# A chunked linear-attention and gated-MLP kernel on one core: 64-bit weights brought to 32 bits by shift, mask and integer add, their range tested on a second load, and an issue order by a finer table of ranks

## The chip, the core and the metric

The kernel runs on one core of a Trainium2 chip. The metric is the device time of one execution in microseconds. Engines: PE is TensorE, DVE VectorE, ACT ScalarE, POOL GpSimd, SP SyncE (here it only issues transfers).

## What is computed

For 4 batches, 8 heads, 768 steps and head size 48, a state of 48 x 48 is carried along:

```python
for t in range(S):
    kt, vt, rt, wt = (k[:, :, t], v[:, :, t], r[:, :, t], w[:, :, t])
    cur = einsum('bhd,bhe->bhde', u[None] * kt, vt)
    y[:, :, t] = einsum('bhd,bhde->bhe', rt, state + cur)
    state = wt[:, :, :, None] * state + einsum('bhd,bhe->bhde', kt, vt)
h = maximum(x @ w_in, 0)                    # x is y as [4, 768, 384], w_in [384, 1024]
conv = sum(conv_w[j] * h[t - 1 + j] for j in 0, 1, 2)
out = (h * sigmoid(conv)) @ w_out           # w_out [1024, 384]
```

`w_in`, `conv_w` and `w_out` arrive as 64-bit floats, the rest as 32-bit ones.

## The kernel before

**Attention.** Each batch is cut into six chunks of 128 steps, 24 in all. `stage_a(n)` loads w, k, r, v of a chunk (192 KB each, in runs of 192 bytes), transposes them on PE (L541), builds running products of w with two scans on DVE (L548, L555), scales k and r by them (L553, L559), and tests w against two bounds on ACT (the guards, L605). `stage_b(n)` makes the scores (L662), masks them by a predicated copy (L666), carries the state (L679, L683, L685) and writes y as a high and a low part into `xT` (L733 or L710, L735 or L711).

**MLP.** `block` takes 384 steps. For each of eight tiles of 128 hidden columns it makes nine products on PE (L755), relu, convolution and gate on ACT and DVE (L767 to L774; the gate is L774), and a high part on ACT and a low part on POOL (L776, L777). Then come three output tiles of 24 products each (L784). There are eight blocks, 64 hidden tiles.

**Weights.** They are used as two 32-bit parts, high and low. They arrive as pairs of 32-bit words, in three groups of `w_in` (`win_pieces`: 384, 384 and 256 columns, each in two halves, one issued by SP and one by ACT) and three of `w_out` (`wout_pieces`). `convert` works on a piece of 128 rows and up to 384 columns; there are 17, 14 wide and 3 of 256 columns. `from_double` takes the exponent (L439 on DVE, L442 on ACT), puts the sign to it (L444, DVE), takes the upper mantissa (L447, DVE), adds the lower word scaled (L450, DVE) and multiplies both on POOL (L453). Then ACT casts the high part (L459) and POOL subtracts for the low one (L460). Raw words lie in the ring of five "gh" slots, in which the hidden tiles lie later, three to a slot.

**The order.** Everything is recorded in `Plan`. `issue` replays it against the durations in `LEN`: whenever an engine is free, it takes the ready operation of lowest rank whose buffers can be had. So each engine's program order is set by ranks. Before, a rank is a formula: `CHUNK` times the chunk, `UNIT` for each hidden tile, `PIECE` for each piece of weights. On the chip the engines run their own lists in order and wait for each other by semaphores.

Of the kernel before, what the change touches and what calls it, by code (L numbers as in the profile page):

```python
# [12 lines left out]
I32 = mybir.dt.int32  # L13
# [11 lines left out]
CHUNK, LEAD, UNIT, DOWN, PIECE = 14.0, 0.0, 5.0, 1.6, 5.0  # L25
FIRST_IN, FIRST_OUT = -10.0, 60.0
AHEAD, GUARD = 10.0, 10.0
# [8 lines left out]
    tr=0.35, kback=0.35, scores=1.1, carried=0.9, state=0.42, y=0.95, mm3=0.53,  # L36
    scan=0.86, small=0.1, pad=0.07, kt=0.47, dg=0.47, cp=0.62, xlo=0.6, sd=0.22, s=0.27,
    stt=0.54, gate=0.47, wts=0.47, wstt=0.47,
    fill=0.25, kh=0.42, guard=0.72, sbd=0.34, xhi=0.49, relu=0.5, mul=0.49, sig=0.43, cast=0.42, out=0.37, exp=0.52,
    z=0.98, diag=1.07, lo=0.97,  # L40
    gather=1.6, carried_rows=1.4, y_rows=1.5,
    load=0.55, issue=0.45, spread=0.64,
)
TAIL = dict(PE=0.22, DVE=0.11, ACT=0.13, POOL=0.07, SP=2.2)
# [66 lines left out]
class Plan:  # L111
# [6 lines left out]
    def op(self, eng, us, f, r=(), w=(), holds=(), moves=0.0, port=False, rank=None):  # L118
        i, deps = len(self.ops), set()
        us = LEN[us] if isinstance(us, str) else us  # L120
# [18 lines left out]
        self.ops.append((eng, us, f, deps, bufs, moves, port, (self.rank if rank is None else rank) + i * 1e-6))  # L139

    def issue(self):
        n = len(self.ops)
        left = [len(o[3]) for o in self.ops]
        users = [[] for _ in range(n)]
        for i, o in enumerate(self.ops):
            for d in o[3]:
                users[d].append(i)
# [5 lines left out]
        for i in range(n):  # L153
            if not left[i]:
                ready[self.ops[i][0]].append((self.ops[i][7], i))
        events, order, t = [], [], 0.0
# [17 lines left out]
        while len(order) < n:  # L174
            for e in engines:
                if free[e] > t:
                    continue
                for k, (_, i) in enumerate(sorted(ready[e])):
                    if places(self.ops[i][4]):
                        break  # L180
                else:
                    continue
                ready[e].remove((self.ops[i][7], i))
                _, us, _, _, _, moves, port, _ = self.ops[i]
                at = t
                if e == "PE" and t < COLD:
                    us *= 1.4
# [5 lines left out]
                free[e] = at + us  # L193
                if moves:
# [5 lines left out]
            assert t < float("inf"), "no order found"  # L200
# [95 lines left out]
def rwkv_conv_moe_kernel(  # L296
# [545 lines left out]
    for n in range(N + 1):  # L842
        if n < N:
# [6 lines left out]
            if f0 < DF:  # L850
                plan.rank = FIRST_IN + PIECE * KT * n
                win_pieces(f0, min(HB, DF - f0), piece, (chunks[n]["w"], 1))
                if n == 0:
                    load_conv()
# [51 lines left out]
```

## Time and profile before

| | |
|---|---|
| runs | 386.19, 386.65, 386.65 us; median 386.65 |
| profiled execution, span | 387.1 us |
| PE busy | 350.6 us (91%), 2790 matmuls |
| DVE, ACT, POOL busy | 281.8, 234.5, 174.6 us |
| HBM read, written | 25.19, 4.72 MB |
| mean granted clock of TensorE | 0.966 |

The span is that of one execution, from its first instruction to its last; it is 0.45 us above the median of the runs. Engines work beside each other, so busy times don't add up. Matmuls overlap: two that follow each other start closer together than one lasts. A row's mean is the length of one instruction; on DVE and ACT too, an instruction that doesn't wait starts some 80 ns before its predecessor's record ends.

### The profile page before, as it was taken

The page shows a single profiled execution, that of the slowest core. Times are in us where ns is not written, and L with a number is a line of the kernel's source. Part 1 is how long each engine was busy: PE and PEld are TensorE (multiplying, and loading weights), DVE is VectorE, ACT ScalarE, POOL GpSimd, SP SyncE. Part 2 cuts the span into 40 slices and gives each one's busy share as a digit, 9 for nine tenths or more (in the row PEclk, how much of TensorE's full clock was granted, in tenths as well). Part 3 has the DMA queues.
Part 4 walks back from the last instruction along what each step waited for, and adds up shares of the span by engine and source line. Part 5 has one row for each costly group of instructions (what it writes and reads, how often), then busy time and mean ns, then how long its engine had stood idle before and what let it go on. Part 6 is the DMA issues. An engine that isn't in the chain of part 4 may idle for free.

```text
span 387.1 us, 7859 instructions
## 1 busy us (share of the span) xinstructions
PE 350.6 (91%) x2790; PEld 320.3 (83%) x2790; DVE 281.8 (73%) x575; ACT 234.5 (61%) x613; POOL 174.6 (45%) x199
## 2 busy tenths in 40 slices
PE   5545978798899999999999999999999999999992
PEld 2435856687688999998999999999999989999992
DVE  4357989999998688578776876688867774656520
ACT  4133766687776565389747663697664725766621
POOL 5265596865785444056443532454544310434320
PEclk9856999899999999999999999999999999999998
DMA  9999984422334354373323447244424130110001
GB/s 150 151 159 179 231 242 98 92 53 49 66 66 99 69 107 78 89 153 85 73 60 75 88 96 143 56 102 94 93 52 94 41 75 10 30 33 20 22 20 69
DMA packets 113571, 34.46 MB, mean 89 GB/s; under 512 B 103069, under 2 KB 110774, under 8 KB 113526
## 3 DMA queue, kind: packets, MB, share of 16 engines
q1 hardware_dynamic: 112852, 32.32, 40.9%
q10 hardware_dynamic: 674, 1.57, 2.0%
q8 instruction: 24, 0.39, 0.4%
q14 instruction: 21, 0.17, 0.1%
HBM read 25.19 MB, written 4.72 MB: 77 GB/s over the span
## 4 chain that ended last, share of the span: by engine, by line
PE 71%; DVE 11%; DMA 5%; issue 3%; SPq 3%; ACT 3%; POOL 2%; ACTq 0%; DVEq 0%; POOLq 0%
PE bank L784 25%; PE bank L755 23%; PE bank L662 6%; PE bank L728 4%; PE bank L541 4%; PE bank L718 4%; PE bank L679 2%; SPq L509 2%; DMA v<-in_v_dram 2%; DMA gh<-in_moe_w_in_dram 2%; PE bank L597 2%; DVE pm L666 1%; DVE a L771 1%; DMA r<-in_r_dram 1%; DVE e L444 1%
## 5 line engine op out<-in xcount | busy, mean ns | idle before, releaser
L755 PE MATMUL bank<-xT,wi 128*128 128x386 f32 x576 | 129.0, 349 | 2.2 <-ACT xT L710 1.7
L784 PE MATMUL bank<-wo,gh 128*128 128x384 f32 x576 | 127.2, 344 | 2.1 <-POOL wo L460 1.7
L777 POOL TENSOR_TENSOR gh<-g,gh 128x384 fp32r<-128x384 f32 x64 | 64.7, 1015 | 114.5 <-ACT gh L776 109.6
L755 PEld LDWEIGHTS bank<-xT,wi 128*128 128x128 f32 x576 | 101.6, 190 | 5.7 <-issue 2.0
L784 PEld LDWEIGHTS bank<-wo,gh 128*128 128x128 f32 x576 | 100.2, 188 | 4.3 <-POOL wo L460 2.0
L769 DVE SCALAR_TENSOR_TENSOR a<-bank,cw,a 128x384 f32<-128x384 f32 x64 | 38.6, 609 | 23.1 <-ACT a L768 22.9
L774 DVE TENSOR_TENSOR g<-bank,a 128x384 f32<-128x384 f32 x64 | 34.8, 549 | 19.0 <-ACT a L773 18.2
L773 ACT ACTIVATE a<-a 128x384 f32<-128x384 f32 x64 | 33.4, 522 | 23.9 <-DVE a L771 23.8
L767 ACT ACTIVATE bank<-bank 128x386 f32<-128x386 f32 x64 | 30.6, 478 | 25.4 <-PE bank L755 24.5
L589 POOL TENSOR_SCALAR_AFFINE_SELECT pm<-dg 128x1024 f32<-128x1024 f32 x24 | 26.2, 1092 | 41.5 <-PE bank L728 39.1
L776 ACT CAST gh<-g 128x384 fp32r<-128x384 f32 x64 | 32.5, 512 | 12.2 <-DVE g L774 12.1
L771 DVE SCALAR_TENSOR_TENSOR a<-bank,cw,a 128x384 f32<-128x384 f32 x64 | 38.8, 611 | 0.8
L666 DVE COPY_PREDICATED pm<-upper,bank 128x512 f32<-128x512 int32 x48 | 33.5, 725 | 5.5 <-PE bank L662 5.2
L768 ACT ACTIVATE a<-bank,cw 128x384 f32<-128x384 f32 x64 | 36.7, 581 | 0.5
L583 POOL TENSOR_TENSOR z<-r,k 128x384 f32<-128x384 f32 x24 | 24.4, 1016 | 12.2 <-DMA r<-in_r_dram 12.2
L548 DVE TENSOR_TENSOR_SCAN kr<-bank,one_end 128x387 f32<-128x387 f32 x24 | 22.9, 956 | 9.2 <-PE bank L541 9.1
L453 POOL TENSOR_TENSOR val<-val,e 128x384 f32<-128x384 f32 (+2 forms) x18 | 16.7, 927 | 19.1 <-DVE val L450 8.0
L585 POOL TENSOR_TENSOR z<-z,ubc 128x384 f32<-128x384 f32 x24 | 24.2, 1008 | 1.2
L662 PEld LDWEIGHTS bank<-kr 48*128 48x128 f32 x288 | 18.4, 188 | 7.0 <-issue 4.1
L662 PE MATMUL bank<-kr 48*128 48x128 f32 x288 | 23.2, 290 | 0.9 <-DVE val L450 0.9
L555 DVE TENSOR_TENSOR_SCAN kr<-bank,dA 128x387 f32<-128x387 f32 x24 | 22.9, 953 | 0.1
L541 PE MATMUL bank<-ident,k 128*128 128x128 f32 x72 | 13.0, 293 | 10.6 <-ACT k L535 10.6
(108 smaller groups left out, 523.7 us busy)
## 6 DMA issues: line engine op xcount, KB each, us to landing
w<-in_w_dram SPq DMA_DIRECT2D x24, 192.0 KB, 3.1
k<-in_k_dram SPq DMA_DIRECT2D x24, 192.0 KB, 3.5
r<-in_r_dram SPq DMA_DIRECT2D x24, 192.0 KB, 3.6
v<-in_v_dram SPq DMA_DIRECT2D x24, 192.0 KB, 3.1
out_dram<-val SPq DMA_DIRECT2D x24, 192.0 KB, 2.0
gh<-in_moe_w_out_dram SPq DMA_DIRECT2D x2, 1152.0 KB, 8.4
last<-kr SPq DMA_DIRECT2D x120, 16.2 KB, 1.8
xT<-xT SPq DMA_DIRECT2D x18, 64.0 KB, 2.4
```

The source lines that it names most:

```text
L662: nc.tensor.matmul(sc[g].t[:, m * L:(m + 1) * L], lhsT=kt(m)[p], rhs=rt(m)[p], start=True, stop=True)
L666: op("DVE", "cp", lambda g=g: nc.vector.copy_predicated(out=pm.t[:, g], mask=upper.unsqueeze(1).to_broadcast([P, NP, L]), data=sc[g].t.rea ...
L755: nc.tensor.matmul(t.t[:, 0:xs.stop - xs.start], lhsT=wi[:, m, a, f * P:(f + 1) * P], rhs=xT[:, x0 + m, c, xs], start=(m == 0 and j == 0), ...
L767: ("ACT", "relu", lambda: nc.scalar.activation(out=h(0, width + 2), in_=h(0, width + 2), func=AF.Relu), [t], [t]),
L768: ("ACT", "mul", lambda: nc.scalar.mul(out=a(), in_=h(1), mul=cw[:, 1, f:f + 1]), [t, "cw"], [a1]),
L769: ("DVE", "stt", lambda: nc.vector.scalar_tensor_tensor(out=a(), in0=h(0), scalar=cw[:, 0, f:f + 1], in1=a(), op0=ALU.mult, op1=ALU.add), ...
L771: ("DVE", "stt", lambda: nc.vector.scalar_tensor_tensor(out=a(), in0=h(2), scalar=cw[:, 2, f:f + 1], in1=a(), op0=ALU.mult, op1=ALU.add), ...
L773: ("ACT", "sig", lambda: nc.scalar.activation(out=a(), in_=a(), func=AF.Sigmoid), [], [a1]),
L774: ("DVE", "gate", lambda: nc.vector.tensor_tensor(out=g.t[:, 0:width], in0=h(1), in1=a(), op=ALU.mult), [t, a1], [g]),
L776: ("ACT", "cast", lambda: nc.scalar.copy(out=part(0)[:, 0:width], in_=g.t[:, 0:width]), [g], [key]),
L777: ("POOL", "lo", lambda: nc.gpsimd.tensor_tensor(out=part(1)[:, 0:width], in0=g.t[:, 0:width], in1=part(0)[:, 0:width].bitcast(F32), op=AL ...
L784: nc.tensor.matmul(acc.t[:, 0:DM], lhsT=part(a)[:, tt * P:(tt + 1) * P], rhs=wo[:, f, c, :], start=(f == 0 and a + c == 0), stop=(f == FT ...
```

## The change

- `convert` no longer goes through the exponent. ACT turns the low word into its top three bits, rounded (a scaled copy to integer), and takes the sign of the high word as 1.0 or -1.0. DVE shifts the high word left by three and masks it (one instruction), and adds the two as integers (another). POOL multiplies by the sign. Cast and low part are as before. Per piece DVE has two instructions instead of four, ACT three instead of two, POOL two as before.
- This holds for magnitudes between 2^-127 and 2. So `in_range` loads all weights a second time (six loads, through the "gh" ring), masks and compares the exponent's upper bits on DVE, and sums up what differs on ACT. The sum joins the guards' flags; if it isn't zero, the general path converts the weights in the old way and computes everything again.
- All halves of `w_in` are issued by SP. `conv_w` is converted as before.
- Ranks come from a table, `RANKS`, with one number for each step of each chunk, piece, hidden tile and output tile. `LEN` has other durations, and PE's operations are charged for a change of their form (`SWITCH`).

```diff
-CHUNK, LEAD, UNIT, DOWN, PIECE = 14.0, 0.0, 5.0, 1.6, 5.0
+DOWN = 1.6
+RANKS = dict(
+    load=[-152.0, -79.7, -8.9, -117.1, -75.2, -21.5, 44.6, 131.8, 85.2, -38.1, -95.7, 157.3, 110.7, 49.5, -13.0,
...
+    range=[150.7, 286.2, 238.8, 120.4, 266.7, 215.2],
...
+def split(val, hi, lo):
+    return (("ACT", "cast", lambda: nc.scalar.copy(out=hi, in_=val())),
+            ("POOL", "lo", lambda: nc.gpsimd.tensor_tensor(out=lo, in0=val(), in1=hi.bitcast(F32), op=ALU.subtract)))
 def convert(raw, hi, lo, n, reads, token):
-    val = Buf(val_k)
-    from_double(raw, lambda: val.t[:, 0:n], n, reads, [val])
+    sign, m, val = Buf(e_k), Buf(wx), Buf(val_k)
+    op("ACT", "cast", lambda: nc.scalar.activation(
+        out=v().bitcast(I32), in_=word(0).bitcast(U32), func=AF.Copy, scale=2.0 ** -29), reads, [val])
+    op("ACT", "cast", lambda: nc.scalar.activation(
+        out=sign.t[:, 0:n].bitcast(F32), in_=word(1), func=AF.Sign), reads, [sign])
+    op("DVE", "wts", lambda: nc.vector.tensor_scalar(
+        out=m.t.bitcast(I32)[:, 0:n], in0=word(1), scalar1=3, scalar2=0x3fffffff, op0=ALU.logical_shift_left,
+        op1=ALU.bitwise_and), reads, [m])
+    op("DVE", "wstt", lambda: nc.vector.tensor_tensor(
+        out=v().bitcast(I32), in0=m.t.bitcast(I32)[:, 0:n], in1=v().bitcast(I32), op=ALU.add), [m], [val])
+    op("POOL", "lo", lambda: nc.gpsimd.tensor_tensor(
+        out=v(), in0=v(), in1=sign.t[:, 0:n].bitcast(F32), op=ALU.mult), [sign], [val], port=True)
...
+def in_range(j, src, n):
+    raw = Buf(again_k)
+    plan.at("range", j)
+    op("SP", "issue", lambda: nc.sync.dma_start(out=raw.t[:, :, 0:2 * n], in_=src), [], [(raw, 0)], [raw],
+       moves=1.05 * 3 * n / HB)
+    op("DVE", "range", lambda: nc.vector.tensor_scalar(
+        out=top(), in0=top(), scalar1=0x78000000, scalar2=0x38000000, op0=ALU.bitwise_and, op1=ALU.bitwise_xor),
+       [(raw, 0)], [raw])
+    op("ACT", "range", lambda: nc.scalar.activation(
+        out=top().bitcast(F32), in_=top(), func=AF.Relu, accum_out=flags[:, 2 * N + j:2 * N + j + 1]), [], [raw])
...
-    for g, (eng, q) in enumerate((("SP", nc.sync), ("ACT", nc.scalar))):
+    for g, (eng, q) in enumerate((("SP", nc.sync), ("SP", nc.sync))):
+        plan.at("rows", 2 * (f0 // HB) + g)
...
-        plan.rank = base + f * UNIT
+        plan.at("hidden", FT * bi + f)
```

The start of SP's list, on which the loads depend (w_120, k_122, r_124 and v_126 to v_128 are the buffers of a chunk's inputs, `gh` raw weights). Before (the other halves of the weights are on ACT's list):

```order
L509 DMA w_120<-in_w_dram 128x8x48
L509 DMA k_122<-in_k_dram 128x8x48
L509 DMA r_124<-in_r_dram 128x8x48
L509 DMA v_126<-in_v_dram 128x8x48
L479 DMA gh<-in_moe_w_in_dram 48x3x768
L483 DMA gh<-in_moe_w_in_dram 16x3x768
L509 DMA w_121<-in_w_dram 128x8x48
L509 DMA k_123<-in_k_dram 128x8x48
L509 DMA r_125<-in_r_dram 128x8x48
L509 DMA v_127<-in_v_dram 128x8x48
L479 DMA gh<-in_moe_w_in_dram 48x3x768
L483 DMA gh<-in_moe_w_in_dram 16x3x768
```

Now:

```order
L633 DMA w_120<-in_w_dram 128x8x48
L633 DMA k_122<-in_k_dram 128x8x48
L633 DMA r_124<-in_r_dram 128x8x48
L633 DMA v_126<-in_v_dram 128x8x48
L633 DMA w_121<-in_w_dram 128x8x48
L633 DMA k_123<-in_k_dram 128x8x48
L633 DMA r_125<-in_r_dram 128x8x48
L633 DMA v_127<-in_v_dram 128x8x48
L603 DMA gh<-in_moe_w_in_dram 48x3x768
L607 DMA gh<-in_moe_w_in_dram 16x3x768
L633 DMA w_120<-in_w_dram 128x8x48
L633 DMA k_122<-in_k_dram 128x8x48
```

Chunk 1's loads moved in front of the first weights, and the two halves of a weight group stand apart on the one queue, with chunk 2 between them.

DVE's list where conversion begins (`val` is the 32-bit value, `e` exponent and sign, `bank` a PSUM bank that holds a step's result, `kr` and `pm` belong to attention). Before:

```order
L586 TENSOR_REDUCE dg_152<-z_151 128x4x2
L439 TENSOR_SCALAR bank_70<-gh 128x384
L447 TENSOR_SCALAR bank_71<-gh 128x384
L450 SCALAR_TENSOR_TENSOR val_72<-gh,bank_71 128x384
L444 SCALAR_TENSOR_TENSOR e_168<-gh,bank_70 128x384
L439 TENSOR_SCALAR bank_66<-gh 128x384
L447 TENSOR_SCALAR bank_71<-gh 128x384
L666 COPY_PREDICATED pm_154<-upper,bank_64 128x512
L444 SCALAR_TENSOR_TENSOR e_169<-gh,bank_66 128x384
L450 SCALAR_TENSOR_TENSOR val_73<-gh,bank_71 128x384
```

Now, later in the list, in front of it the front part of four chunks instead of one:

```order
L717 TENSOR_REDUCE dg_153<-z_151 128x4x2
L688 TENSOR_TENSOR kr_133<-bank_67,kr_133 128x3x128
L555 TENSOR_SCALAR bank_65<-gh 128x384
L555 TENSOR_SCALAR bank_70<-gh 128x384
L558 ISA val_72<-bank_65,val_72 128x768
L558 ISA val_73<-bank_70,val_73 128x768
L671 MEMSET bank_71 128x4
L803 COPY_PREDICATED pm_155<-upper,bank_68 128x512
L777 TENSOR_SCALAR sd_161<-s_163,last_139 112x48
L555 TENSOR_SCALAR bank_65<-gh 128x384
```

The pair of a shift (L555) and an add (L558, printed as an ISA instruction over 768 halves) stands where four instructions stood, and it comes behind more of the attention.

## Rows read from the trace of the kernel before

**Rows 1.** The page, part 2: busy tenths in 40 equal slices of the span, for TensorE (PE) and VectorE (DVE), and the mean busy share of the 16 DMA engines.

```profile
PE   5545978798899999999999999999999999999992
...
DVE  4357989999998688578776876688867774656520
...
DMA  9999984422334354373323447244424130110001
```

**Rows 2.** Busy time of each engine in five stretches of the run. Columns: stretch and its length in us; busy us of PE, PEld (weight load), DVE, ACT, POOL with the number of instructions; then the granted clock of TensorE as a share of full speed, the busy share of the DMA engines, and GB/s.

```profile
0.00:40.00 40.00, 21.43 (x124) 16.24 (x126) 21.25 (x49) 13.80 (x42) 19.72 (x43) 0.74 1.06 159
...
40.00:107.00 67.00, 56.55 (x518) 48.38 (x517) 65.03 (x143) 48.62 (x137) 46.69 (x50) 0.97 0.50 117
...
107.00:150.00 43.00, 42.49 (x364) 38.44 (x364) 35.41 (x73) 28.92 (x80) 22.00 (x23) 1.00 0.41 86
...
150.00:350.00 200.00, 200.00 (x1619) 187.44 (x1619) 146.84 (x289) 127.01 (x325) 78.06 (x77) 1.00 0.35 76
...
100.00:120.00 20.00, 17.82 (x138) 15.28 (x138) 19.88 (x40) 15.17 (x38) 16.26 (x17) 1.00 0.37 76
```

**Rows 3.** The chain that ended last, from 300 us on: start in us, length in us, what. L541 is a transpose, L662 scores, L718 the carried part of y, L728 the part within the chunk, L755 hidden products, L784 output products; the last row is the store of the last output rows.

```profile
303.74 0.98 PE bank L541 x9
...
316.33 1.09 PE bank L662 x16
...
318.01 1.06 PE bank L718 x8
...
319.40 1.01 PE bank L728 x16
...
348.40 1.06 PE bank L755 x6
...
368.03 10.94 PE bank L784 x63
...
379.49 1.86 DMA out_dram<-val
```

**Rows 4.** Instructions on DVE in order of time, around 105.8 us: start, length, line, operation, tiles. This is the eighth gate.

```profile
105.77 0.55 DVE L774 TENSOR_TENSOR g<-bank,a 128x384 f32<-128x384 f32 x1
```

**Rows 5.** Instruction groups on DVE over the whole run, shapes kept apart: line, engine, operation, out<-in, form, count | busy us, mean ns of one | idle us before them and what ended it. L439 to L450 are conversion, the others attention.

```profile
L439 DVE TENSOR_SCALAR bank<-gh 128x384 int32<-128x384 int32 x14 | 7.7, 547 | 5.6 <-DMA gh<-in_moe_w_in_dram 5.6
...
L450 DVE SCALAR_TENSOR_TENSOR val<-gh,bank 128x384 f32<-128x384 uint32 x14 | 7.6, 541 | 0.0
...
L439 DVE TENSOR_SCALAR bank<-gh 128x256 int32<-128x256 int32 x3 | 1.2, 412 | 0.0
...
L555 DVE TENSOR_TENSOR_SCAN kr<-bank,dA 128x387 f32<-128x387 f32 x24 | 22.9, 953 | 0.1
...
L553 DVE TENSOR_TENSOR kr<-bank,kr 128x384 f32<-128x384 f32 x24 | 13.2, 549 | 2.0 <-PE bank L541 1.5
...
L666 DVE COPY_PREDICATED pm<-upper,bank 128x512 f32<-128x512 int32 x48 | 33.5, 725 | 5.5 <-PE bank L662 5.2
...
L735 DVE TENSOR_TENSOR xT<-bank,xT 112x512 fp32r<-112x512 f32 x20 | 13.7, 685 | 11.9 <-ACT xT L733 11.9
...
L685 DVE COPY s<-bank 112x192 f32<-112x192 f32 x4 | 1.4, 342 | 0.0
```

**Rows 6.** Instructions on DVE in order of time, two that stand back to back.

```profile
67.31 0.55 DVE L439 TENSOR_SCALAR bank<-gh 128x384 int32<-128x384 int32 x1
67.78 0.55 DVE L447 TENSOR_SCALAR bank<-gh 128x384 int32<-128x384 int32 x1
```

**Rows 7.** Instruction groups on ACT, columns as in the DVE groups: the exponent step wide and narrow, the cast, a guard and the read of its sum.

```profile
L442 ACT ACTIVATE bank<-bank,ebias 128x384 int32<-128x384 int32 x14 | 7.7, 551 | 7.1 <-DVE bank L439 6.9
...
L442 ACT ACTIVATE bank<-bank,ebias 128x256 int32<-128x256 int32 x3 | 1.3, 436 | 0.0
...
L459 ACT CAST wi<-val 128x384 fp32r<-128x384 f32 x6 | 3.0, 504 | 0.3 <-POOL val L453 0.2
...
L605 ACT ACTIVATE junk<-w,guard_hi 128x384 bf16<-128x384 f32 x24 | 14.8, 617 | 0.0
...
L605 ACT ACTIVATION_READ_ACCUMULATOR junk<-w,guard_hi 128x1 f32 x24 | 4.6, 191 | 0.0
```

**Rows 8.** Instruction groups on POOL, columns as before: the last multiplication of a conversion.

```profile
L453 POOL TENSOR_TENSOR val<-val,e 128x384 f32<-128x384 f32 x14 | 14.1, 1004 | 17.8 <-DVE val L450 7.3 <-DMA r<-in_r_dram 6.6 <-DVE e L444 3.5
```

**Rows 9.** SP's issues in order of time: start, time that SP spent on it, line, destination and source.

```profile
9.02 7.59 SPq L509 DMA_DIRECT2D r<-in_r_dram  x1
...
20.24 5.56 SPq L509 DMA_DIRECT2D r<-in_r_dram  x1
...
35.82 0.51 SPq L509 DMA_DIRECT2D v<-in_v_dram  x1
```

**Rows 10.** All engines in order of time, three instructions with the idle time of their engine before them and what ended it in brackets.

```profile
17.39 0.56 DVE L439 TENSOR_SCALAR bank<-gh 128x384 int32<-128x384 int32 x1 [5.57 <-DMA gh<-in_moe_w_in_dram]
...
25.99 0.27 ACT L535 COPY k<-k 128x96 f32<-128x96 f32 x1 [4.83 <-DMA gh<-in_moe_w_in_dram]
...
34.70 0.27 ACT L535 COPY k<-k 128x96 f32<-128x96 f32 x1 [3.07 <-DMA v<-in_v_dram]
```

**Rows 11.** DMA issues by line: destination and source, queue, count, KB each, median us from issue to landing.

```profile
v<-in_v_dram SPq DMA_DIRECT2D x24, 192.0 KB, 3.1
...
gh<-in_moe_w_out_dram SPq DMA_DIRECT2D x2, 1152.0 KB, 8.4
```

More of the change, by code (lines that the diff above doesn't have):

```diff
@@ L35 @@
 LEN = dict(
[L36 to L40, printed above, removed]
+    tr=0.3, kback=0.3, scores=0.93, carried=0.8, state=0.6, y=1.0, mm3=0.53,
+    scan=0.875, small=0.1, pad=0.07, kt=0.465, dg=0.44, cp=0.62, xlo=0.6, sd=0.3, s=0.265,
+    stt=0.527, gate=0.465, wts=0.461, wstt=0.461,
+    range=1.25, fill=0.172, kh=0.335, guard=0.61, sbd=0.364, xhi=0.483, relu=0.41, mul=0.475, sig=0.426, cast=0.418, out=0.375,
+    exp=0.48, z=0.97, diag=1.06, lo=0.966,
     gather=1.6, carried_rows=1.4, y_rows=1.5,
@@ L44 @@
+FULL, TRANS, ROW, COL = range(4)
+MODE = dict(tr=TRANS, kback=TRANS, gather=TRANS, carried=TRANS, carried_rows=TRANS, scores=ROW,
+            state=COL, y=COL, y_rows=COL)
+SWITCH = {(FULL, ROW): 0.17, (TRANS, ROW): 0.17, (COL, ROW): 0.17, (FULL, COL): 0.11, (TRANS, COL): 0.11,
+          (FULL, TRANS): 0.08, (COL, TRANS): 0.05}
 TAIL = dict(PE=0.22, DVE=0.11, ACT=0.13, POOL=0.07, SP=2.2)
@@ L138, in op, with reset, run @@
                     t.kind.wanted += 1
[L139 to L147, printed above, removed]
+        self.ops.append((eng, us, f, deps, bufs, moves, port, self.rank + i * 1e-6, mode))
+    def reset(self):
+        kinds, stores = {}, {}
+        for o in self.ops:
+            for x in o[4]:
+                kinds[id(x.kind)] = x.kind
+        for k in kinds.values():
+            k.held = k.served = k.wanted = 0
+            stores[id(k.places)] = k
+        for k in stores.values():
+            if not hasattr(k, "all"):
+                k.all = list(k.places)
+            k.places[:] = k.all
+        seen = set()
+        for o in self.ops:
+            for x in o[4]:
+                if id(x) not in seen:
+                    seen.add(id(x))
+                    x.t, x.uses, x.turn = None, 0, x.kind.wanted
+                    x.kind.wanted += 1
+                x.uses += 1
+    def run(self, ranks):
+        self.reset()
+        ops, n = self.ops, len(self.ops)
+        left = [len(o[3]) for o in ops]
         engines = ("PE", "DVE", "ACT", "POOL", "SP")
@@ L154, in issue @@
             if not left[i]:
-                ready[self.ops[i][0]].append((self.ops[i][7], i))
-        events, order, t = [], [], 0.0
+                heapq.heappush(ready[ops[i][0]], (ranks[i], i))
+        events, order, t, end, mode = [], [], 0.0, 0.0, FULL
         def places(bufs):
@@ L213, in issue, with general @@
                         b.kind.places.append(b.t)
-                for u in users[i]:
+                for u in self.users[i]:
                     left[u] -= 1
                     if not left[u]:
-                        ready[self.ops[u][0]].append((self.ops[u][7], u))
+                        heapq.heappush(ready[ops[u][0]], (ranks[u], u))
+        return order, end
+    def issue(self):
+        ops, n = self.ops, len(self.ops)
+        self.users = [[] for _ in range(n)]
+        for i, o in enumerate(ops):
+            for d in o[3]:
+                self.users[d].append(i)
+        ranks = [o[7] for o in ops]
+        order, end = self.run(ranks)
         self.order = order
         for _, i in order:
-            for b in self.ops[i][4]:
+            for b in ops[i][4]:
                 if b.kind.make and not b.made:
                     b.t, b.made = b.kind.make(), True
-            self.ops[i][2]()
-def general(ctx, tc, r, k, v, w, u, out, const, ident, x, moe_block):
+            ops[i][2]()
+def general(ctx, tc, r, k, v, w, u, out, const, ident, x, weights, moe_block):
     nc = tc.nc
@@ L669, in stage_b @@
         if c < NCH - 1:
+            plan.at("state", n)
             t = Buf(pb)
```

222 lines of the change are left out of this document (155 added, 67 removed), and 4 rows, old and new, of the table hidden.

## Prediction

> **What bounds the kernel now.** I read the page first [rows 1]: the row of TensorE (PE) is full at the end but not in its first ten slices, while the DMA row stands at 9 for six slices and the DVE row fills from the fifth. So I cut the run by stages [rows 2]. Up to 40 us PE is busy 21.4, DVE 21.3, ACT 13.8, and the DMA engines are full: this stage waits for transfers. From 40 to 107 us DVE is busy 65.0 of 67 us, PE 56.6, ACT 48.6, POOL 46.7: VectorE sets the pace. From 107 us on PE is busy 42.5 of 43 and 200.0 of 200 us: from there the end is fixed by the PE work that is left, at paces that rows at the end of the chain show (six hidden products in 1.06 us, 63 output products in 10.94) and about 8 us behind the last matmul [rows 3]. The mark that I use for the change of stage is the gate of the eighth hidden tile on DVE, 105.77 us [rows 4]. A microsecond by which the same state comes earlier is a microsecond of the end. A microsecond taken from DVE, ACT or POOL after it is worth nothing: in 150 to 350 us they idle 53, 73 and 122 of 200 us [rows 2].
>
> The program is judged by its profiled execution, 387.1 us of span; the median of the runs is 386.65, so I subtract from 386.65.
>
> **Conversion on DVE.** A piece had four DVE instructions and now has two. Wide ones last 541 to 547 ns, narrow ones 412 [rows 5], but back to back they start 0.47 us apart [rows 6], so I price all DVE work at its row less 0.08. Up to the eighth gate the order before has 65 conversion instructions (16 pieces and the first one of the next), the order now 34, which are all 17 pieces: 31 fewer, 25 wide at 0.46 and 6 narrow at 0.33, 13.5 us. But the new order places more in front of that gate: one second scan (0.87), two products with keys and receptances (0.93), one masked copy (0.62), one low part of x (0.60), one copy of a state (0.26) [rows 5]: 3.3 us. Net 10.2 us. DVE was busy 85.1 us up to the gate (21.25 + 65.03 - 1.2), and will be 74.9.
>
> The new add is the unknown price. The order shows it as one ISA instruction over 768 halves, not 384 words. Nearest rows: a two-operand instruction of 384 words, 0.54 us; a straight line through 256 and 384 words (0.412, 0.547) gives 0.95 us at 768 steps [rows 5]. I take 0.54, because the words are the same bytes as in the rows, and keep 0.95 for the range: 14 x 0.40 + 3 x 0.27 = 6.4 us. Here a rule of the Trainium skill speaks against the change: "VectorE: DVE Perf Modes", section "The perf-mode tier table", puts a two-tensor operation with any operand in PSUM at one element a cycle, and the masked word lies in a PSUM bank. By that rule the add would be the slow one; by "What auto-detection actually checks" on the same page, all operands of 16 bits with step one give two a cycle, and the add costs what a word add costs. No run here shows either yet.
>
> **Conversion on ACT and POOL.** A piece had an exponent and a cast on ACT and now has a scaled copy, a sign and a cast. Rows for such forms are 0.50 and 0.55 [rows 7]; back to back I take 0.47, with 0.42 and 0.58 as bounds. Up to the gate it is 51 instead of 33 instructions, 8.3 us, and two more guards (0.8 each with their read [rows 7]): ACT rises from 62 us (13.8 + 48.6 [rows 2]) to 72. The order shows one table load, as before, so the sign function brings no reload. POOL keeps two instructions for a piece (1.0 us each [rows 8]); with one more piece in front of the gate it stands at 68. So DVE falls to 75 and the other two rise to 72 and 68. This is why I don't count the whole relief.
>
> **The loads.** Now the first weight rows stand fifth on SP, with half of them on the ACT queue at the same time. SP then blocks for 7.59 and 5.56 us issuing r loads [rows 9], DVE waits 5.57 us for weight rows, ACT 4.83 and 3.07 us with PE behind it [rows 10]. In the new order chunks 0 and 1 go first, and the load of v for chunk 3 and the last part of the first weight group are within the first 20 transfers: 16 loads of 192 KB and 384 x 384 weights of 8 bytes, 4.3 MB. At 159 GB/s (0 to 40 us [rows 2]) that is 27 us, with 1 us before and 2 to 3 behind it about 30. Now v of chunk 3 is issued at 35.82 and lands some 3.1 us later [rows 9, 11], at 39. So attention is fed 9 us earlier. Weight groups two and three come later in SP's list than now (some 7.7 MB up to their end, 48 us at the same rate); in the new order the fourth hidden tile, the first that needs them, stands behind 52 us of DVE work, which covers it. If that cover went (DVE idle below 5 us), they would cost up to 5 us. The six transfers moved from ACT to SP cost SP 0.4 to 0.7 us each of issue, while SP waits for full queues anyway.
>
> **DVE's idle time.** Up to the gate DVE idles 20.7 us now, 18.75 of them before 40 us [rows 2]. Nine go with the earlier loads. Against this I add 5 for waits among three engines that are now nearly equally long, between 0 (DVE idles 2.0 of 67 us today with the others at 73%) and 15. Taken: 16.7. Low end 8 (beside the nine, nearly 4 more of the present wait of 5.57 for weight rows [rows 10] go, and nothing is added), high end 27 (none of the nine gained, 6 more). The gate comes at 74.9 + 16.7 = 91.6, 14.2 earlier than now; by the ends at 83 or 102.
>
> I give no credit for the clock: PE was granted 0.74 of full speed on average in the first 40 us [rows 2], so part of that time was at its lower level of 1.2 GHz, while it was busy about half the time. Denser chunks could lift that, but PE is not what ends the first stage.
>
> **PE after the gate.** At the gate the orders stand alike on PE: eight hidden tiles, seven chunks' scores, 18 output products before and 15 now, within 1 us. From there the new order puts 57 output products and two chunks in front of the ninth tile, about 20 us for PE at the paces of [rows 3], against 18 us for DVE. So the 2 us that PE lost between 100 and 120 us (17.82 busy of 20 [rows 2]) go too.
>
> **Range test.** Six loads, 6.3 MB, each with a DVE instruction of 1152 columns (by the line above 1.36 us) and an ACT one (line through 436 and 551 ns: 1.24, and 0.19 for the read [rows 7]): 7.7 us of DVE and 8.2 of ACT, all behind the eighth gate, in the idle time named above. Price 0. Without that cover the first would cost 1.4 us, all six 8. Finer ranks elsewhere I price at 0: PE has no idle time there to win.
>
> Sum: 386.65 - 14.2 - 2 = 370.4, say **370 us**. Unknowns: gate at 83 gives 361, at 102 gives 380.
>
> **Rivals.**
> - *The relief goes to ACT and POOL* (14%). For: 72 and 68 us of work, and a piece now starts on ACT, goes to DVE, POOL, ACT, POOL. ACT idles 44 of the first 107 us now; if 30 stay, the gate is at 102 and the time 380. Against: much of ACT's idling is the wait for DVE and for loads.
> - *The add runs one half-word a step* (11%): in that sense the change does not do what it says. 6.4 us more on DVE, gate at 98, time 376.8. For: the order's 768. Against: same bytes.
> - *Loads and balance work fully* (12%): gate at 83, 361 us.
> - *Slower, by the slots* (6%). Each range load takes one of the five "gh" slots that the hidden tiles and output products turn over in. It is held from issue to the end of the ACT read: 8.4 us of landing [rows 11] and 2.8 of work, some 11 us, and on SP the loads of chunks queue behind one that waits for its slot. If PE stood through half of each hold, 6 x 5.5 = 33 us, the time would be 403. It decides from 16.2 / 6 = 2.7 us of PE idle for each. Against: two groups of three hidden tiles fill less than the five slots most of the time, and from 107 us on PE shows no idle time that a slot could explain.
> - *No change* (2%): gains and losses cancel.
>
> **Numbers.** Forecast (365 to 375) 55%, the rest as given. About 0.2% is what a measurement of this kernel can tell from no change; faster by more than that 0.92, within 0.02, slower 0.06. The range 360 to 380 takes in the bounds of idle time and add, and about half of the first rival.
>
> **What would show it.** Right: eighth gate at 88 to 95 us; DVE busy about 75 up to it, ACT about 72; the add near 0.54 us; v of chunk 3 landed by 31 us; PE full from then on, with DVE idle from 150 to 350 us some 8 us less than now. The loads step is wrong if DVE idles over 20 us up to the gate; the DVE step if the add takes 0.9 us. Gaps on PE in front of output products, with SP waiting at a range load, would be the slots. A hidden tile that waits for its second weight group would be the order of loads.

## The result and the profile after

The changed kernel takes 372.69 us in the median (371.11, 371.33, 374.05, 374.12): 0.9633 of the time before, interval 0.9595 to 0.9671. Run once more beside the experiments it took 371.79 (0.9617, 0.9566 to 0.9668). Forecast were 370.0, range 360 to 380.

The stages [rows 2] now, same columns; the first two rows are cut at the eighth gate:

```profile
0.00:40.00 40.00, 33.48 (x336) 27.32 (x336) 30.67 (x69) 25.76 (x85) 26.54 (x50) 1.00 1.02 181
40.00:91.63 51.63, 45.59 (x336) 39.35 (x332) 45.42 (x94) 42.96 (x114) 39.78 (x43) 0.90 0.68 164
...
107.00:150.00 43.00, 43.00 (x353) 40.05 (x348) 32.54 (x64) 33.27 (x82) 17.25 (x17) 1.00 0.69 179
150.00:350.00 200.00, 199.00 (x1578) 187.51 (x1578) 148.98 (x290) 132.28 (x328) 80.27 (x80) 1.00 0.33 74
100.00:120.00 20.00, 19.83 (x198) 17.45 (x196) 16.98 (x36) 14.22 (x41) 7.63 (x9) 1.00 0.69 172
```

In the first 40 us PE and DVE do half as much again as before and ACT nearly twice as much, while the DMA engines are as full; from 107 us on PE is full as before. The eighth gate [rows 4], on DVE:

```profile
91.63 0.55 DVE L915 TENSOR_TENSOR g<-bank,a 128x384 f32<-128x384 f32 x1
```

It stands 14.14 us earlier. From it to the end of the span it was 281.3 us (387.1 - 105.77) and is 277.8 (369.4 - 91.63). The two profiled spans differ by 17.7 us, the medians by 14.0: a run's time is 1.7 us more than its span (371.11 against 369.4), so the profiled execution before was a longer one of its kind, and that of the change a shorter one. A second profiled execution of the change has the gate at 91.98 us.

The instructions of the conversion [rows 5, 7, 8] and of the range test (L575, L578), over the whole run:

```profile
L558 DVE CUSTOM_DVE_ANT_0 val<-bank,val 128x768 uint16<-128x768 uint16 x14 | 7.6, 549 | 1.3 <-ACT val L551 1.0
L555 DVE TENSOR_SCALAR bank<-gh 128x384 int32<-128x384 int32 x14 | 7.4, 550 | 1.7 <-DMA gh<-in_moe_w_in_dram 1.7
L575 DVE TENSOR_SCALAR gh<-gh 128x1152 int32<-128x1152 int32 x5 | 4.9, 988 | 3.0 <-DMA gh<-in_moe_w_out_dram 3.0
L558 DVE CUSTOM_DVE_ANT_0 val<-bank,val 128x512 uint16<-128x512 uint16 x3 | 1.3, 418 | 0.4 <-ACT val L551 0.4
```

```profile
L551 ACT ACTIVATE val<-gh 128x384 int32<-128x384 uint32 x14 | 7.6, 549 | 5.2 <-DMA gh<-in_moe_w_in_dram 5.2
L578 ACT ACTIVATE gh<-gh 128x1152 f32<-128x1152 int32 x5 | 6.4, 1272 | 0.5 <-DVE gh L575 0.5
```

The integer add over 768 halves takes 549 ns. Of the loads [rows 9], v of chunk 3 is now issued at 19.22 us and landed at 25.05; before it was issued at 35.82 and landed at 40.95:

```profile
19.22 3.09 SPq L633 DMA_DIRECT2D v<-in_v_dram  x1
```

### The profile page after: what moved, and what is told of

Read it like the earlier page. It is cut to its first block, busy times and chain, and to the rows that moved or that the text cites. A ratio compares the mean times of both kernels' runs of the same rounds, so it can differ in the third digit from the quotient of the medians.

```text
span 369.4 us, 7909 instructions
## 1 busy us (share of the span) xinstructions
PE 348.0 (94%) x2790; PEld 318.8 (86%) x2790; DVE 272.0 (74%) x547; ACT 246.5 (67%) x642; POOL 175.8 (48%) x199
## 4 chain that ended last, share of the span: by engine, by line
PE 62%; DMA 13%; SPq 6%; ACT 5%; POOL 5%; DVE 4%; issue 3%; DVEq 0%; ACTq 0%; POOLq 0%
PE bank L896 23%; PE bank L925 21%; DMA w<-in_w_dram 5%; PE bank L798 4%; PE bank L868 4%; PE bank L665 4%; DMA r<-in_r_dram 3%; DMA gh<-in_moe_w_in_dram 3%; PE bank L858 3%; SPq L706 3%; SPq L633 2%; PE bank L817 2%; DMA last<-kr 1%; PE bank L730 1%; ACT e L553 1%
## 5 line engine op out<-in xcount | busy, mean ns | idle before, releaser
L896 PE MATMUL bank<-xT,wi 128*128 128x386 f32 x576 | 127.1, 354 | 0.4 <-DVE val L558 0.4
L925 PE MATMUL bank<-wo,gh 128*128 128x384 f32 x576 | 118.8, 342 | 0.6 <-POOL wo L540 0.3
L910 DVE SCALAR_TENSOR_TENSOR a<-bank,cw,a 128x384 f32<-128x384 f32 x64 | 38.4, 611 | 33.8 <-ACT a L909 33.5
L914 ACT ACTIVATE a<-a 128x384 f32<-128x384 f32 x64 | 32.9, 521 | 16.8 <-DVE a L912 16.7
L917 ACT CAST gh<-g 128x384 fp32r<-128x384 f32 x64 | 31.9, 510 | 12.2 <-DVE g L915 11.9
L912 DVE SCALAR_TENSOR_TENSOR a<-bank,cw,a 128x384 f32<-128x384 f32 x64 | 38.2, 609 | 0.4
L673 DVE TENSOR_TENSOR_SCAN kr<-bank,one_end 128x387 f32<-128x387 f32 x24 | 22.9, 956 | 8.9 <-PE bank L665 8.8
L684 DVE TENSOR_TENSOR_SCAN kr<-bank,dA 128x387 f32<-128x387 f32 x24 | 22.9, 955 | 0.3
L868 PE MATMUL bank<-pm,v 128*48 128x128 f32 x320 | 21.9, 277 | 0.0
L868 PEld LDWEIGHTS bank<-pm,v 128*48 128x48 f32 x320 | 16.8, 124 | 3.9 <-issue 2.5
```

Source lines behind the costliest of these rows:

```text
L868: nc.tensor.matmul(y.t[rows, cs], lhsT=vf[:, h * D:h * D + rows.stop - rows.start], rhs=pm.t[:, g, m, :], start=(c == 0 and m == 0), stop= ...
L896: nc.tensor.matmul(t.t[:, 0:xs.stop - xs.start], lhsT=wi[:, m, a, f * P:(f + 1) * P], rhs=xT[:, x0 + m, c, xs], start=(m == 0 and j == 0), ...
L910: ("DVE", "stt", lambda: nc.vector.scalar_tensor_tensor(out=a(), in0=h(0), scalar=cw[:, 0, f:f + 1], in1=a(), op0=ALU.mult, op1=ALU.add), ...
L912: ("DVE", "stt", lambda: nc.vector.scalar_tensor_tensor(out=a(), in0=h(2), scalar=cw[:, 2, f:f + 1], in1=a(), op0=ALU.mult, op1=ALU.add), ...
L914: ("ACT", "sig", lambda: nc.scalar.activation(out=a(), in_=a(), func=AF.Sigmoid), [], [a1]),
L917: ("ACT", "cast", lambda: nc.scalar.copy(out=part(0)[:, 0:width], in_=g.t[:, 0:width]), [g], [key]),
```

## Experiments

In nine of the twelve only what is named was changed and the order of all other instructions held fixed on every engine; in the other three, which say so, the planner laid out the order anew. With the order held PE issues the same 2790 matmuls in the same order, and the delay of any one can be read: its start less its start in the profile of the change. The delays, in us, worked out from the traces, at the first product of hidden tiles 1, 5, 8, 9, 16, 32 and 48. Delays and gate are those of one profiled execution, the time is the median of all runs; the profiled execution was 2.6 us longer than the median without the range test, 1.6 longer with more DVE, 2.4 shorter with one DVE op, elsewhere within 0.5.

| kernel | 1 | 5 | 8 | 9 | 16 | 32 | 48 | eighth gate | time |
|---|---|---|---|---|---|---|---|---|---|
| change, again | 1.0 | 0.5 | 0.2 | 0.3 | 0.3 | 1.8 | 1.3 | 91.98 | 371.79 |
| one DVE op, late | 0.1 | 0.1 | 0.3 | 0.4 | 0.4 | 0.7 | 0.8 | 92.08 | 372.10 |
| one DVE op | -0.1 | 0.6 | 3.6 | 2.9 | 2.9 | 2.7 | 2.6 | 94.83 | 375.93 |
| no range test | 2.9 | 2.8 | 2.0 | 4.2 | 4.2 | 4.2 | 4.3 | 92.94 | 375.37 |
| more POOL | 3.1 | 3.7 | 8.2 | 10.5 | 10.5 | 11.2 | 11.4 | 99.64 | 382.12 |
| more ACT | 2.5 | 4.9 | 9.7 | 11.3 | 11.3 | 13.7 | 13.4 | 103.22 | 383.90 |
| former loads | 14.4 | 14.5 | 13.9 | 13.8 | 13.8 | 15.4 | 15.3 | 105.49 | 386.11 |
| more DVE | 7.1 | 9.0 | 15.0 | 15.5 | 15.5 | 16.9 | 16.8 | 107.07 | 386.27 |
| former arithmetic | 3.4 | 7.5 | 14.9 | 16.0 | 16.0 | 17.4 | 17.5 | 107.94 | 388.11 |

A delay arises in front of the eighth or ninth tile and then stays within 2.5 us up to the end.

**The conversion taken back, order laid out anew.** `convert` with the former steps (`any_double`, `split`); the ranks stay, so the planner lays out another order.

> The changed kernel (372.7 us) with the former conversion of the pieces: four DVE instructions, an exponent and a cast on ACT for each; loads, ranks and range test of the change stay. My theory: the relief of VectorE is the larger part of the gain. All 17 pieces stand in front of the eighth gate, so 34 DVE instructions of 0.33 to 0.46 us come back there, 14 to 15 us, while ACT gives up 17 of 0.47; DVE idles 15.5 us up to the gate now and can hide a part. Expected: gate at 98 to 103 instead of 91.6, time 379 to 384. Rival A (the earlier loads and the order made the gain, DVE work hides in its idle time): gate within 3 us of 91.6, time under 376. Rival B (relief and loads multiply, everything lost without the relief): 386 or more.

407.44 us, 1.0514 (1.0475 to 1.0553) of the kernel before. The gate came at 98.5, in the range expected, but in this order 14 of the 17 pieces are through DVE in front of it and 12 masked copies instead of 14, so it marks another state. Then PE idled 14 us between 140 and 200 us. SP's waits from 90 to 200 us (what it waited for, total, count, longest):

```profile
SPq L944 <- ACT val L943: 13.8, 3, 9.7
SPq L621 <- PE bank L653: 13.3, 6, 5.9
```

L944 is the store of output rows: three stores wait in SP's list for their rows, and the loads of chunks (L621) stand behind them. So the run tells of another order, not of the conversion.

**The former transfers of w_in, order laid out anew.**

```diff
-    rows=[6.9, -54.1, 13.8, 33.0, 19.6, 17.4, ...],
+    rows=[-151.0, -151.0, -79.6, -79.6, -8.8, -8.8, ...],
-        for g, (eng, q) in enumerate((("SP", nc.sync), ("SP", nc.sync))):
+        for g, (eng, q) in enumerate((("SP", nc.sync), ("ACT", nc.scalar))):
```

> The changed kernel with the former transfers of the w_in rows: each group's first half behind the loads of one chunk on SP, its second half on the ACT queue at the same time, released by the first guard; new conversion, ranks and range test stay. My theory: v of chunk 3, which landed at 25 us in the changed kernel and at 39 in the kernel before, lands again after 33 us; DVE starves up to 40 us, 5 to 9 us more of it are lost and the gate comes 5 to 9 us later, time 378 to 382. Rival A (the order of loads is worth little, since weights that come early let conversion start early): time within 2 us of 372.7. Rival B (early weights help the new conversion): under 371.

397.06 us, 1.0255 (1.0226 to 1.0284) of before; gate 110.3, and PE idled 5 us between 160 and 180 us. Worse than all three theories, and again another order. The later experiments therefore hold the order.

**No range test.**

```diff
-    op("SP", "issue", lambda: nc.sync.dma_start(out=raw.t[:, :, 0:2 * n], in_=src), ...)
+    op("SP", "issue", lambda: None, ...)      # and so for its DVE and ACT operation
```

> The changed kernel without the range test: the six loads, the six DVE and six ACT instructions are left out (the range of weights isn't tested in it); the order of all else is the same, row for row. My theory: all of it stands behind the eighth gate beside a full PE, price 0; at most the 1.0 us that PE idles between 240 and 250 us comes back: 371.5 to 373. Rival A (slots of gh held by range loads, SP queue blocked by them): 3 us or more faster. Rival B (6.3 MB of transfers slow the chunk loads from 90 us on): 1 to 3 us faster, with PE idle time between 90 and 250 us gone.

375.37 us, not faster. It was 2.9 us late already at the first hidden product, 44 us before the change starts its first range instruction on DVE (92.1 us), and from the ninth tile on the delay stays at 4.0 to 4.3 while the change still does most of its range test. The 1 us that PE idles between 240 and 250 us is there without the test too. Price 0; where the 4 us come from is under clock, below.

**The new conversion alone in the kernel before, order laid out anew.** Its `convert` has the new steps. The ranks are the former formula, but the planner lays out another order from them.

> The kernel before (386.65 us) with the new conversion of the pieces alone: two DVE, three ACT and two POOL instructions for each; its loads, its ranks and no range test (so the range of weights isn't tested). My theory: up to the eighth gate 16 pieces and one instruction lose 31 to 33 DVE instructions, 13 us of DVE work; the loads leave DVE starving up to 40 us as now, so what was 65 us of DVE work behind 40 us shrinks by about 10 (some of the pieces stand in front of 40 us): gate 96 to 99 instead of 105.8, time 377 to 380. Rival A (ACT and POOL take the relief): gate 102 or later, time 383 or more. Rival B (the conversion is all of the gain): 372 to 374.

383.25 us, 0.9913 (0.9880 to 0.9946): 3.4 us faster. My theory fell; rival A has the time. But the loads aren't the former ones: in the order laid out anew, two loads of `w_out` stand in front of those of chunk 3.

```profile
28.35 1.06 SPq L511 DMA_DIRECT2D gh<-in_moe_w_out_dram  x2
43.89 0.91 SPq L526 DMA_DIRECT2D v<-in_v_dram  x1
```

v of chunk 3 was issued at 43.89 us instead of 35.82 and landed at 47.55 instead of 40.95. And the profiled execution took 388.58 us, the longest of the five. Its stages up to the gate at 104.09:

```profile
0.00:40.00 40.00, 23.41 (x151) 17.58 (x152) 18.74 (x46) 16.88 (x50) 19.10 (x43) 0.79 1.06 184
40.00:104.09 64.09, 55.21 (x460) 48.39 (x459) 57.09 (x114) 51.17 (x147) 50.81 (x53) 0.92 0.49 104
```

DVE works 75.8 us instead of 85.0 and idles 28.3 instead of 20.7: in this execution most of the relief turns into idle time. How much of that the later loads of chunk 3 make, the run doesn't tell; with the loads truly as before, the new conversion alone may be worth more than 3.4 us.

**The former arithmetic in the new order.** The former six operations stand in the places of the new ones. Its last DVE read of raw words can come after their slot has been given on, so some pieces hold other values; its time is read.

```diff
+        def first():
+            nc.vector.tensor_scalar(out=ex(), in0=word(1), scalar1=20, scalar2=0x7ff, ...)
+            nc.scalar.activation(out=ex(), in_=ex(), func=AF.Relu, scale=2.0 ** 23, bias=ebias)
+            nc.vector.tensor_scalar(out=m.t.bitcast(I32)[:, 0:n], in0=word(1), scalar1=0xfffff, scalar2=0x100000, ...)
+        def second():
+            nc.vector.scalar_tensor_tensor(out=v(), in0=word(0).bitcast(U32), scalar=2.0 ** -32, ...)
+            nc.vector.scalar_tensor_tensor(out=ex(), in0=word(1), scalar=-2 ** 31, in1=ex(), ...)
+        op("DVE", "wts", first, reads, [m])
+        op("DVE", "wstt", second, [m], [val])
```

> The changed kernel with the former arithmetic of the pieces (four DVE instructions, an exponent and a cast on ACT), put into the places of the new one, so that every other instruction keeps its order on every engine. In the run with the former conversion before this one the scheduler had laid out everything anew, and PE stood idle for 15 us between 140 and 200 us behind chunk loads, in SP's order; this one takes that away. My theory: 34 DVE instructions more, 15 us of which DVE's idle time up to the gate (15.5) hides under half: gate 6 to 10 us later, time 378 to 383. Rival A (the order and the loads are nearly all of the gain): under 376. Rival B (without the relief nothing is left, as 407 us in the run before suggests): 386 or more.

388.11 us, 1.0017 (0.9990 to 1.0045): nothing of the gain is left; rival B has the time. Gate at 107.94, DVE busy 95.6 us up to it:

```profile
0.00:40.00 40.00, 32.07 (x269) 26.15 (x270) 31.15 (x71) 22.23 (x72) 24.31 (x47) 0.91 1.00 180
40.00:107.94 67.94, 52.06 (x400) 44.22 (x398) 64.46 (x127) 41.95 (x109) 43.92 (x47) 0.87 0.51 126
```

The stand-in is dearer than the former conversion. It keeps the exponent in SBUF, where the kernel before has it in a PSUM bank, and two of its four instructions are longer (768 and 676 ns, against 538 and 547):

```profile
L564 DVE SCALAR_TENSOR_TENSOR e<-gh,e 128x384 int32<-128x384 int32 x14 | 10.8, 768 | 0.0
L555 DVE TENSOR_SCALAR e<-gh 128x384 int32<-128x384 int32 x14 | 9.5, 676 | 0.0
```

Over the 17 pieces that is 22.9 us instead of 17.6, 5.3 more. By the 0.87 us of delay for a us of DVE work that the run with more DVE gives below, some 4.6 us of the delay of 16.3 (an estimate) belong to the stand-in, and nearly 12 to the former arithmetic: most of the gain, not surely all of it.

**The former loads in the new order.** After planning, the twelve transfers are moved behind the loads of chunks 0, 1 and 2.

```diff
+        order = [o for o in order if o[1] not in self.marked]
+        for g in range(3):
+            k = 1 + max(n for n, o in enumerate(order) if o[1] in self.loaded[g])
+            order[k:k] = [(order[k][0], i) for i in moved if self.marked[i] == g]
```

> The changed kernel with the transfers of w_in moved ahead on SP: each group behind the loads of chunk 0, 1 and 2, where they stood in the kernel before, all on SP; every other instruction keeps its order on every engine. In the order of the change v of chunk 3 is 19th with some 1 MB of weights ahead of it, here 28th with 3.1 MB: at 170 GB/s 12 us later, 37 instead of 25. My theory (chunks first is worth 9 us of starvation): PE and DVE idle 6 to 12 us more up to 40 us, gate 5 to 10 us later, time 378 to 383. Rival A (PE catches up, since weights are early): within 2 us of the changed kernel. Rival B (the order behind it was laid out for the later weights and breaks): 386 or more.

386.11 us, 0.9968 (0.9938 to 0.9998): again nearly nothing is left. That is the time of rival B, which gave as its reason an order laid out for later weights. v of chunk 3 landed at 38.27 us, 13.2 later, and the first hidden product came 14.4 later. The stages up to the gate:

```profile
0.00:40.00 40.00, 24.56 (x156) 18.09 (x156) 16.68 (x40) 13.29 (x45) 15.98 (x39) 0.85 1.00 170
40.00:105.49 65.49, 58.09 (x513) 51.20 (x512) 59.87 (x123) 55.33 (x153) 50.18 (x53) 0.94 0.54 136
```

DVE does 14.0 us less in the first 40 us, and that is the whole delay.

**More work on each engine in turn.** The shift three times, the sign three times, the low part twice.

```diff
+        op("DVE", "wts", lambda: [nc.vector.tensor_scalar(...) for _ in range(3)], reads, [m])
+        op("ACT", "cast", lambda: [nc.scalar.activation(..., func=AF.Sign) for _ in range(3)], reads, [sign])
+        op(e2, us2, lambda: [f2() for _ in range(2)], [val, token], [(token, 1)], port=True)
```

> The changed kernel with the shift and mask of every piece issued three times instead of once, same result, same order of all else: 34 DVE instructions of 0.33 to 0.46 us more, 15 us, all in front of the eighth gate, ACT and POOL as in the change. My theory (DVE paces the stage): as with the former arithmetic or a little more, because ACT keeps its 17 instructions: gate 6 to 11 us later, time 378 to 384. Rival A (DVE's idle time hides it): under 376. Rival B (ACT's load is what counts, then this one is as good as the change and the one with the former arithmetic better).

> The changed kernel with the sign of every piece taken three times instead of once, same result and order: 34 ACT instructions of 0.42 to 0.48 us more, 15 us, in front of the eighth gate; ACT is busy 69 of the 92 us there. Theory (DVE paces, ACT has 23 us idle and stands in the chain of each piece): a part comes through, gate 3 to 8 us later, time 375 to 380. Rival A (all three engines pace in turn: any 15 us comes through whole, as on DVE): time 384 or more. Rival B (ACT's idle time hides it): under 374.

> The changed kernel with the low part of every piece computed twice on POOL, same result and order: 17 POOL instructions of 1.0 us more, 17 us, in front of the eighth gate; POOL is busy 67 of the 92 us there. Theory (POOL has 25 us idle, and the low part ends a piece that the products wait for): gate 3 to 8 us later, time 375 to 380. Rival A: any 15 us comes through whole, 385 or more. Rival B (POOL's idle time hides it): under 374.

Up to the gate DVE had 17.7 us more (93.8 against 76.1), ACT 17.1 (85.8 against 68.7), POOL 13.5 (79.8 against 66.3); the gate came 15.4, 11.6 and 8.0 us later: 0.87, 0.68 and 0.59 us for one. The times are 386.27, 383.90 and 382.12 us. On DVE that is more than my theory (6 to 11 us), and no rival had it; for ACT and POOL it is more than my theory, and for ACT nearly rival A: none has slack that hides work, though they idle 23 and 25 us. (POOL has 15.7 us more over the whole run, some of it behind the gate; its delay ends at 10.5 at the ninth tile.)

**One DVE instruction for a piece, twice.** First with the low word in SBUF and the instruction early, then with the low word in a PSUM bank and the instruction where the add stood.

```diff
+            nc.scalar.activation(out=m.t[:, 0:n], in_=word(0).bitcast(U32), func=AF.Copy, scale=-0.936 * 2.0 ** -51, bias=-2.0)
+            nc.vector.scalar_tensor_tensor(out=v().bitcast(I32), in0=word(1), scalar=3, in1=m.t.bitcast(I32)[:, 0:n],
+                                           op0=ALU.logical_shift_left, op1=ALU.bitwise_xor)
```

> The changed kernel with one DVE instruction for a piece instead of two: ACT writes the low word as a float between -2 and -2 - 7.5 x 2^-22, whose bits are 0xC0000000 plus three low bits, and DVE shifts the high word left by three and XORs it with them (the two leading ones of an in-range word cancel; the value is then within 2^-23 of the 64-bit weight). ACT and POOL keep their counts, the order of all else is the same. 17 DVE instructions of 0.33 to 0.46 us fewer, 7.5 us, all in front of the eighth gate. Theory from the last runs (34 more DVE instructions moved the gate by 15.1 us, 0.9 us for a us, so DVE paces the stage): gate 5 to 8 us earlier, 84 to 87 us, time 364 to 367. Rival A (DVE and the loads stand level, as more of either takes all the gain: relieving one alone gives little): gate 89 to 92, time 369 to 372. Rival B (the order no longer fits): slower than 372.

375.93 us: my theory fell, rival B has the time. The instruction took 773 ns and DVE waited for ACT; in the second version it took 552 ns:

```profile
L560 DVE SCALAR_TENSOR_TENSOR val<-gh,val 128x384 int32<-128x384 int32 x14 | 10.8, 773 | 8.1 <-ACT val L554 6.1 <-DMA last<-kr 1.7
```

```profile
L575 DVE SCALAR_TENSOR_TENSOR val<-gh,bank 128x384 int32<-128x384 int32 x14 | 7.7, 552 | 5.7 <-ACT bank L570 3.3 <-DMA last<-kr 2.3
```

> The version with one DVE instruction for a piece, mended in the two points that its trace shows: ACT writes the low word to a PSUM bank instead of the value's SBUF tile (with both inputs in SBUF the shift and XOR took 773 ns, with one in PSUM such an instruction took 541 in the kernel before), and the DVE instruction stands where the add of the change stood, not where the shift and mask stood (there DVE waited 6.1 us for ACT). ACT and POOL keep their counts, the order of all else is that of the change. DVE then has 17 instructions of 0.33 to 0.46 us fewer up to the eighth gate, 7.3 us, without a new wait. Theory A (the pace is set by whichever engine is late at each piece, so that a microsecond added anywhere comes through at 0.6 to 0.9, but one taken from DVE alone gives at most half, as ACT and POOL stay): gate 88 to 91, time 368 to 371. Theory B (symmetric: 0.9 a microsecond): gate 85 to 87, time 364 to 366. Theory C (other limits stand level already, PE is busy 80 of 92 us): gate 91 to 94, time 371 to 374, no difference.

372.10 us, 0.9607 (0.9569 to 0.9644), against 371.79 (0.9617) of the change: no difference. Up to the gate at 92.08:

```profile
0.00:40.00 40.00, 33.96 (x331) 27.85 (x333) 29.25 (x66) 25.41 (x84) 26.34 (x50) 1.00 1.02 180
40.00:92.08 52.08, 43.99 (x345) 38.00 (x340) 39.93 (x80) 42.66 (x115) 39.96 (x43) 0.93 0.68 164
```

DVE is busy 69.2 us instead of 76.1, and the gate is where it was: theory C. Part of the relief went into waits that this form brings: DVE idles 6.5 us in front of the 17 instructions, 4.1 of it for ACT's copy (two of these copies stand later in ACT's list than in the change), where the change idles 3.4 us in front of its 34, 1.5 of it for ACT. No version beat the change.

**The change once more.**

> The changed kernel once more, as the measure for the runs beside it. Expected: 371 to 374, in two groups about 3 us apart as in its first four runs (371.1, 371.3 at a mean granted clock of 0.98; 374.1, 374.1 at 0.975). If the two groups come from the clock in the 40 to 80 us stretch, the longer ones show a lower clock there and the same work behind it.

371.24, 371.39, 372.2, 373.57: no two groups here. Its clock was 0.67 in 20 to 30 us where the change's first profile had 1.00, and higher from 40 to 80, so the lower clock is not tied to the stretch that I named.

## Why the prediction held, and what was wrong in it

**The mark.** Right. In the fixed order the end of the span comes 277 to 281 us after the eighth gate in nine of ten kernels, whether the gate stands at 91.6 or at 107.9 (in the tenth, without the range test, 283.3). The delays in the table go through to the end.

**The term of 2 us behind the gate.** Wrong, though it came out. Of the 2.2 us that PE lost between 100 and 120 us, 1.7 lay in front of the gate at 105.77 and were in the 14.2 already; behind the gate PE idled 0.5 us in all, and in the change it idles 1.4. Still the stretch from the gate to the end is 3.6 us shorter, because the orders don't stand alike on PE at the gate, "within 1 us", as I had it: by then PE has done 667 matmuls instead of 629, and 268.9 us of its work are left instead of 273.8. That the sum came so near is luck in this term.

**The sizes.** Gate 91.6 forecast, 91.63 measured. DVE busy 74.9 and idle 16.7 forecast, 76.1 and 15.5 measured: the two misses of 1.2 us cancel, and the 5 us for waits were a choice between 0 and 15, so the agreement to 0.03 us is luck. ACT 72 and 68.7, POOL 68 and 66.3. The add 0.54 and 0.549 us, though one operand lies in PSUM: of the two rules of the Trainium skill, "VectorE: DVE Perf Modes", the one on 16-bit operands ("What auto-detection actually checks") agrees with this, the tier table's does not. v of chunk 3 was forecast at 30 and landed at 25.05; the first 40 us moved 181 GB/s, not the 159 that I took. The time came out 2.7 us over the forecast, within the range.

**The sum was of the wrong kind.** I wrote "net 10.2 us" for the conversion and nine for the loads, less 5 for waits, as terms that add. In the order of the change they are two conditions that must both hold:

| eighth gate, us | weights between chunks 0, 1, 2, as before | chunks first |
|---|---|---|
| former conversion | 105.77 (former order) | 107.94 (new order; stand-in, see above) |
| new conversion | 105.49 (new order) | 91.63 (new order) |

In the new order, taking the loads back costs 13.9 us and taking the conversion back up to 16.3, each about all of the 14.1. With the weights early, DVE's relief becomes idle time, since work reaches it late (16.68 us of work in the first 40 instead of 30.67). With the former conversion, early inputs meet a DVE that needs 95.6 us of work (93.8 where the shift was tripled, with its results in PSUM, and the gate came at 107.07). As an account of the end state the terms hold (DVE has 9.0 us less work and 5.2 less idle time up to the gate), but in this order neither is to be had without the other, and the rivals, which let one term fail and kept the rest, gave 376.8 or 380 us where the runs give 386 to 388.

Outside that order it is open. The new conversion in the kernel before brought 3.4 us, though chunk 3's loads came 6.6 us later than before. No run has both parts in the former order, so what the new order is worth by itself isn't known, nor what a planner could make of one part alone: an order made for the change loses with either part gone, and that some of this is a misfit of the order isn't excluded.

**The bound.** "VectorE sets the pace" was half right. Work added to DVE comes through at 0.87, but 6.9 us taken away brought nothing (with some 3 us of new waits): in the change DVE stands at the corner where it has stopped being the only bound. The rival of relief that goes to ACT and POOL named the right neighbours (work added there comes through at 0.68 and 0.59), but not their price: the gate came at 91.6, not at 102. The chain that ended last, followed back from the end of the run, shows it. Of the stretch from 40 us to the gate it spends on each, in us (the rest are issues and SP):

| kernel | DVE | ACT | POOL | PE | transfers |
|---|---|---|---|---|---|
| before | 35.2 | 6.2 | 7.2 | 9.0 | 4.3 |
| former arithmetic | 40.3 | 2.7 | 5.2 | 7.4 | 5.0 |
| more DVE | 31.9 | 4.0 | 1.0 | 15.4 | 7.1 |
| more ACT | 4.4 | 50.3 | 1.0 | 0.0 | 2.6 |
| more POOL | 5.7 | 5.8 | 35.2 | 8.7 | 0.0 |
| change | 1.5 | 13.7 | 8.2 | 1.6 | 20.8 |
| change, again | 12.8 | 13.4 | 5.0 | 4.7 | 7.4 |
| one DVE op, late | 2.8 | 16.5 | 10.0 | 2.2 | 13.8 |

Before, and wherever DVE has more work again, DVE holds about half of the chain. In the change it holds 1.5 us in one execution and 12.8 in the other, and ACT, POOL and the transfers hold the rest: which of them ends a wait last differs between two executions of one program. That is how 6.9 us less on DVE can bring nothing. Releasers are inferred, so these figures are rough, and no run relieves ACT, POOL or the transfers alone.

**The range test.** Price 0, as forecast, and the slots didn't bind. But my sign for it was wrong: it runs from 92.1 to 160.5 us, and DVE's idle time from 150 to 350 us fell by 2.1 us, not 8. I had its instruction at 1.36 us; it took 0.99.

**The clock.** I gave no credit. Granted were 1.00 in the first 40 us (0.74 before), but 0.90 from there to the gate (0.97). In the run without the range test it was 0.66 from 20 to 30 us and 0.83 from 100 to 110, where the change's profile has 1.00 in both; that this makes its 4 us, and the spread of the change from 371 to 374 (granted mean 0.98 and 0.975), fits, but no run sets the clock by itself. And its loads were late: v of chunk 2, issued at 14.71 us (14.66 in the change), landed at 21.60 instead of 18.91, v of chunk 3 at 27.75 instead of 25.05, the last part of w_in at 48.16 instead of 45.27. These 2.7 to 2.9 us are as much as the first hidden product was late, so for that part late loads are the nearer cause; why they were late isn't shown.

## What to carry to other kernels

In a fixed order two reliefs can each be a condition for all of the gain; price each part with the others in place and without them, before adding terms. To price one part of a scheduled program, hold the issue order and read the delay of the same instruction along the run; where the order is laid out anew, the run prices another program, and can move loads that the edit doesn't name. A stand-in for former steps must put its results where they lay before, or it has another price. Idle time of an engine in a chain of several is not slack: adding work costs 0.6 to 0.9 of itself there, while taking work away may bring nothing. Follow the chain back in two executions before calling one engine the bound.

## What the hardware showed that I had not expected

DVE instructions that work in SBUF alone were lengthened by POOL. In the first version with one instruction for a piece, both inputs in SBUF, the four wide ones without a POOL instruction beside them took 543 to 558 ns; of the ten with one, two took 559 and eight 585 to 1234. With one input in PSUM all fourteen took 527 to 557, POOL busy or not. The range test, with one input, from SBUF to SBUF, took 753 and 764 ns for 1152 columns without POOL, 853 with POOL beside it for a quarter of the time, and 1196 and 1376 with POOL beside it throughout. The Trainium skill, "SBUF — State Buffer", section "Who interferes with whom", says that a DVE instruction with two SBUF inputs contends with a POOL instruction that reads SBUF; the trace agrees in eight of the ten. That sentence isn't about the range test, which has one input. The scratch in PSUM banks avoids it: the shift of the change, from SBUF to PSUM, took 537 to 561 ns for 384 columns, POOL busy or not, and the stand-in's exponent step, from SBUF to SBUF, 344 to 354 in five (POOL beside one of them) and 494 to 1085 in the nine others, all with POOL beside them.
